# Seven half products in place of eight in the first MLP product of the last three blocks

## The chip, the cores and the metric

The kernel runs on 1 core of one Trainium2 chip. The metric is the device time of one execution in microseconds (us): 1153.07 us is the median of 3 runs of the kernel before, 1152.66 the lowest and 1155.45 the highest. The profile shows one further execution, taken by the hardware profiler.

The engines are named as the profile names them: PE is TensorE (matmuls), DVE is VectorE, ACT is ScalarE, POOL is GpSimd, SP is SyncE, which issues nearly all transfers (DMA). PSUM is the memory that PE writes to, in eight banks of 128 x 512 fp32.

## The reference, cut to what matters

Two layers, each an attention over 8 neighbours at distances 0, 2, ..., 14, and a mixer with an MLP, on x of 2048 rows and 512 columns:

```python
def A(x):                       # attention, 32 heads of 16
    q, k, v = split(x @ wqkv)
    logits = einsum(q, k[pos - 2 * w]) * 16 ** -0.5     # w = 0..7
    return einsum(softmax(logits), v[pos - 2 * w]) @ wo

def B(x):
    h = gelu(layernorm(x) @ w1)
    x1 = x + shift_quarters(h) @ w2
    return x1 + gelu(layernorm(x1) @ w3) @ w4           # w3 512 x 1792

x = x + A(layernorm(x));  x = x + B(layernorm(x))       # twice
```

The product with w3 is the one that the change computes in another way.

## The kernel before, in words

**Tiles and steps.** Each layer is done in 4 blocks of 512 rows, so there are eight steps n = 0..7, called blocks here; 4 to 7 are the second layer. A block goes through `p1_stream` (layer norm, product with wqkv, result to DRAM), `p2` (attention on DVE, four units of 8 heads, each a multiplication, a reduction, a softmax, a second multiplication and a tree of additions over 128 x 4096 elements), `p3` (product with wo, norm, product with w1, gelu), `p4` (product with w2, norm, result turned into the tile nT) and `p5` (the MLP). The work of up to three blocks is interleaved: `p5` of block n runs beside `p2` of block n+1 or n+2.

**Precision.** Every fp32 operand is split into an f16 high and an f16 low half, and a product is the sum of three f16 matmuls (`HLS`, l.40). So 128 columns of w3 times 512 rows, over 4 parts of the contraction, are 12 matmuls 128x512.

**The MLP, `p5` (l.1342).** A group of 3, 4 or 5 row tiles of 128 rows (5 in block 7; the fifth is done as a product 128 wide from a tile xt) passes 14 chunks of 128 columns of w3. Per chunk c: the first product (`up`, 12 matmuls into one of four PSUM banks "mm"); ACT's gelu in that bank and its copy as high half g; the low half by DVE, or by ACT and POOL; the second product (`down`, 3 matmuls for each row tile into four banks "acc"). w3 and w4 were split once by `big_pair` (l.932), stored to DRAM, and are loaded again for each block (`w<-w`) into 8 slots.

**Scales.** `p4` scales the normed rows to `SN` = 1024 before they become f16; each chunk of w3 has a scale of its own (`power_of`, l.503).

**What sets the order.** Every operation is recorded in a graph and then issued in one fixed list of numbers, `ORDER` (l.44): number // 4 is the operation, number % 4 the engine among its alternatives. `SLOTS` (l.220) gives each tile its place in memory. `plan` (l.311) replays the list, and `InOrder` (l.339) keeps each engine's instructions in exactly that order. No engine can pass over an instruction that waits. All instructions carry the line number of the one helper that issues them, l.348 before (l.372 after), so groups in the profile are told apart by tile names: `mm<-nT,w` is the first MLP product, `acc<-w,g` the second, `prod<-kv,q` attention, `mm<-wo_hl,oT` the product with wo.

The loop that sets the stages (l.1421 on) calls `p3`, `p4`, `p5` for n = 0..7 and, from n = 1 on, `p1_stream` and `p2` of n + 3 behind them; the list then moves the operations.

Of the kernel before, what the change touches and what calls it, by code (L numbers as in the profile page):

```python
# [1462 lines left out]
```

## Time and profile before

| | |
|---|---|
| median of 3 runs | 1153.07 us |
| the profiled execution's own time | 1153.17 us |
| its span | 1151.4 us |
| PE busy | 1138.7 us (99%) |
| DVE busy | 890.5 us (77%) |
| ACT busy | 600.7 us (52%) |
| POOL busy | 389.2 us (34%) |
| first MLP product `mm<-nT,w`, 128x512 | 1176 matmuls, 266.1 us |
| second MLP product `acc<-w,g`, 128x512 | 1302 matmuls, 298.1 us |

The profiled execution's own time is 1.8 us longer than its span, and both differ from the median by less than the runs do from each other. In the timeline a row is a run of like instructions: start, busy time, engine, operation, out<-in, shape, count; the brackets give idle time ahead of it and what ended that. In a list of groups the columns are: count | busy time in us, mean ns of one | idle time before them and its releasers. In the table of windows each engine has its busy time in a stretch, with the number of its instructions.

### The profile page before, as it was taken

The numbers are of one execution on the slowest core, as the hardware profiler recorded it, in microseconds if no ns is written. First come the engines' busy times: TensorE is split into PE (matmuls) and PEld (weight loads), VectorE is DVE, ScalarE is ACT, GpSimd is POOL, SyncE is SP. The second block draws the span as 40 slices with busy tenths as digits, with TensorE's granted clock in tenths as the row PEclk, the third lists the DMA queues.
The fourth block names the chain that finished last, engine by engine and source line by source line (L and its number), as shares of the span: only waits on it lengthen the run. The fifth ranks groups of instructions, "written<-read, shape, count | busy, mean of one in ns | idle before, by whom it ended". The sixth has DMA issues, their size and how long they took to land.

```text
span 1151.4 us, 15775 instructions
## 1 busy us (share of the span) xinstructions
PE 1138.7 (99%) x5661; PEld 558.4 (49%) x5661; DVE 890.5 (77%) x1077; ACT 600.7 (52%) x1156; POOL 389.2 (34%) x474
## 2 busy tenths in 40 slices
PE   8999999999999999999999999999999999999998
PEld 7555555555444444444444444444444444444554
DVE  6889989999998994699948998899835999324112
ACT  6776677556645555264644554635444544344232
POOL 4464354224325235402323563431512242323000
PEclk9999999999999999999999999999999999999999
DMA  7789987753875645862677679764457646533232
GB/s 247 235 251 286 276 260 242 247 206 101 247 201 148 209 102 146 241 201 73 187 186 252 187 194 227 180 169 133 116 163 200 221 108 197 124 83 101 74 110 73
DMA packets 237270, 207.35 MB, mean 180 GB/s; under 512 B 109388, under 2 KB 162884, under 8 KB 237192
## 3 DMA queue, kind: packets, MB, share of 16 engines
q1 hardware_dynamic: 236096, 205.51, 62.3%
q8 instruction: 44, 0.72, 0.2%
q10 hardware_dynamic: 1096, 0.85, 0.2%
q14 instruction: 34, 0.28, 0.1%
HBM read 141.03 MB, written 39.47 MB: 157 GB/s over the span
## 4 chain that ended last, share of the span: by engine, by line
PE 79%; DVE 10%; DMA 4%; issue 3%; POOL 2%; ACT 2%; SPq 0%; DVEq 0%; POOLq 0%; ACTq 0%
PE mm L348 55%; PE acc L348 25%; DVE prod L348 4%; DVE L L348 2%; DMA kvq_d<-ev 1%; POOL g L348 1%; DMA w<-in_A_x_dram 1%; DVE g L348 1%; DMA kv<-kvq_d 1%; DVE mx L348 1%; DMA w<-w 1%; DVE wq_hl L348 0%; DVE x L348 0%; SPq L348 0%; DVE f L348 0%
## 5 line engine op out<-in xcount | busy, mean ns | idle before, releaser
L348 PE MATMUL acc<-w,g 128*128 128x512 f16 x1302 | 298.1, 379 | 0.0
L348 PE MATMUL mm<-nT,w 128*128 128x512 f16 (+1 forms) x1344 | 294.8, 372 | 1.8 <-ACT ev L348 0.8
L348 POOL TENSOR_TENSOR g<-f,g 128x512 f16<-128x512 f32 (+1 forms) x123 | 173.0, 1412 | 330.8 <-ACT g L348 156.9
L348 ACT ACTIVATE mm<-mm,s_w 128x512 f32<-128x512 f32 (+2 forms) x158 | 98.2, 622 | 253.8 <-PE mm L348 253.3
L348 PEld LDWEIGHTS <-w 128*128 128x128 f16 x1512 | 140.9, 98 | 154.2 <-issue 3.3
L348 PEld LDWEIGHTS <-g 128*128 128x128 f16 x1398 | 136.7, 98 | 157.0 <-POOL g L348 0.2
L348 PE MATMUL mm<-wq_hl,xt 128*128 128x512 f16 x744 | 166.3, 379 | 0.6 <-DMA xt<-g 0.4
L348 PEld LDWEIGHTS <-xt 128*128 128x128 f16 x1008 | 98.6, 98 | 117.3 <-issue 1.4
L348 DVE TENSOR_REDUCE L<-prod 128x128 f32<-128x2048 f32 (+1 forms) x44 | 142.8, 3248 | 0.4
L348 DVE TENSOR_TENSOR prod<-kv,q 128x4096 f32<-128x4096 f32 (+1 forms) x27 | 100.8, 3736 | 10.5 <-DMA q<-kvq_d 5.9
L348 DVE TENSOR_TENSOR prod<-prod 128x1024 f32<-128x1024 f32 (+2 forms) x56 | 91.0, 1626 | 0.9
L348 PE MATMUL mm<-nT,w_hl 128*128 128x512 f16 x384 | 86.0, 379 | 0.5 <-DVE g L348 0.5
L348 PE MATMUL mm<-wo_hl,oT 128*128 128x512 f16 x384 | 86.0, 379 | 0.0
L348 PE MATMUL mm<-w_hl,h 128*128 128x512 f16 x384 | 85.5, 379 | 0.0
L348 DVE SCALAR_TENSOR_TENSOR g<-mm,c_g,g 128x512 f16<-128x512 f32 (+1 forms) x53 | 39.1, 742 | 56.5 <-ACT g L348 56.4
L348 DVE TENSOR_TENSOR prod<-kv,L 128x4096 f32<-128x4096 f32 (+1 forms) x21 | 77.5, 3690 | 0.4
L348 ACT ACTIVATE g<-mm,c_g 128x512 f16<-128x512 f32 (+1 forms) x112 | 74.5, 671 | 2.1
L348 PEld LDWEIGHTS <-oT 128*128 128x128 f16 x426 | 41.6, 98 | 49.6
L348 PE MATMUL acc<-wq_hl,xt 128*128 128x512 f16 x264 | 59.7, 379 | 0.0
L348 PEld LDWEIGHTS <-w_hl 128*128 128x128 f16 x384 | 37.5, 98 | 45.8 <-issue 0.8
L348 PEld LDWEIGHTS <-h 128*128 128x128 f16 x384 | 37.5, 98 | 45.2 <-DVE h L348 0.4
L348 DVE SCALAR_TENSOR_TENSOR x<-mm,s_wo,x 128x512 f32<-128x512 f32 x32 | 23.8, 747 | 41.2 <-PE mm L348 37.7
(245 smaller groups left out, 1364.1 us busy)
## 6 DMA issues: line engine op xcount, KB each, us to landing
w<-w SPq DMA_DIRECT2D x224, 256.0 KB, 3.9
kv<-kvq_d SPq DMA_DIRECT2D x62, 768.0 KB, 4.9
kvq_d<-ev SPq DMA_DIRECT2D x84, 256.0 KB, 4.0
w<-in_B_w_dram SPq DMA_DIRECT2D x28, 256.0 KB, 4.6
w<-g SPq DMA_DIRECT2D x28, 256.0 KB, 5.8
q<-kvq_d SPq DMA_DIRECT2D x28, 256.0 KB, 3.1
w<-in_A_x_dram SPq DMA_DIRECT2D x16, 256.0 KB, 5.1
x<-in_A_x_dram SPq DMA_DIRECT2D x16, 256.0 KB, 4.8
```

The costliest lines, as they stand in the source:

```text
L348: i = f(*a, **k).ins
```

## The change

For blocks 5, 6 and 7 (`FEW`) the first MLP product takes two chunks of w3 at once, a matrix of 256 columns by 512 parts of the contraction, halved in both directions, against rows halved in both directions. It is done in the form of Strassen and Winograd: seven products of halves in place of eight. Each product is 6 matmuls 128x256. The parts are:

- `lower_rows` and `turn_half`, in `p4`: four half-width subtractions of normed row tiles for each of two pairs of tiles, on DVE or POOL, their split into f16 halves, and their transposing DMAs into a tile S/U.
- `weight_sums`, behind block 3's MLP: w3 is read again, each pair of chunks gives two sums and differences of halves, these are split and stored in DRAM (`w34s`).
- `pair_up`, in `p5`: loads the two sums of a pair, and makes the seven products in two "mm" banks X and Y. ACT copies X out as s and, after an addition, half of Y as u; DVE does three additions 128x256 in PSUM (`Y += s`, `X += u`, `Y += s`), between which PE goes on writing to the same banks.
- The tiles S/U of block 5 lie in a "kv" slot and its weight sums in "w" slots; those of blocks 6 and 7 lie in the space of wq_hl, which is free after block 7's product with wqkv (`ends=wq_users` makes the DMAs that fill it wait for that).
- Scales: 512 in place of 1024 for the rows, and one scale for both chunks of w3 in a pair.
- `ORDER`, `SLOTS` and the place of 26 fill matmuls at the start (`KEEP`) are new throughout.

PE's instructions by kind: `mm<-nT,w` 128x512 from 1176 to 672; 882 matmuls 128x256 new (`nT,w` 336, `wq_hl` 168, `nT,wq_hl` 168, `kv,w` 126, `wq_hl,w` 84); fp32 turns `mm<-ident,f` from 100 to 120; `nT,minus_id` from 3 to 4. DMAs: 14 reads of w3, 14 writes and 42 loads of weights come, 12 transposes for S/U; five row tiles fewer are turned by DMA.

```diff
+    FEW = (5, 6, 7)
+    HOME = {5: ("kv", "f32", "f32", "f32", "f32", "w"), 6: ("nS", "ev", "xt", "ev", "xt", "ws"), 7: ("nS", "q", "o", "ev", "xt", "ws")}
...
-24 16 404 408 40 32 48 45 29 60 36 20 56 52 688 684 400 64 1788 69 72 1772 196 76 208 202 108 114 204 116 214 120 2316
+16 40 24 404 408 45 32 29 48 60 36 20 56 52 692 684 400 64 1772 69 77 196 72 202 108 114 121 204 116 80 210 214 86 126
...
-KEEP = {33: 26}
+KEEP = {22: 26}
...
+    def lower_rows(n, k, key, nr):
+        if k < 2 or k >= NT:
+            firsts[n][k] = nr
+            return
+        up, j, Q = firsts[n][k - 2], k - 2, D // 2
+        e, u = [Buf(b) for b in HOME[n][1:3]]
+        ev, uv = lambda: f32s(e), lambda: f32s(u)[:, :Q]
+        either(key, lambda E: E.tensor_sub(ev()[:, :Q], nr.t[:, :Q], up.t[:, :Q]), [nr, up], [(e, 0)])
+        either(key, lambda E: E.tensor_sub(ev()[:, Q:], nr.t[:, Q:], ev()[:, :Q]), [nr, (e, 0)], [(e, 1)])
+        either(key, lambda E: E.tensor_sub(uv(), up.t[:, Q:], ev()[:, Q:]), [up, (e, 1)], [u])
+        either(key, lambda E: E.tensor_sub(nr.t[:, :Q], nr.t[:, Q:], nr.t[:, :Q]), [], [nr])
...
+    def weight_sums(c, key):
+        either(key, lambda E: E.tensor_add(e.t[:, :Q], v(cd)[:, :Q], v(cd)[:, Q:]), [cd], [(e, 0)])
+        either(key, lambda E: E.tensor_sub(e.t[:, Q:], e.t[:, :Q], v(ab)[:, :Q]), [(e, 0), ab], [(e, 1)])
+        either(key, lambda E: E.tensor_sub(v(cd)[:, :Q], v(ab)[:, :Q], v(cd)[:, :Q]), [ab], [cd])
+        either(key, lambda E: E.tensor_sub(v(cd)[:, Q:], v(ab)[:, Q:], e.t[:, Q:]), [ab, (e, 1)], [cd])
...
+    def pair_up(n, c, key, w3):
+        X, Y_, s, u = Buf("mm"), Buf("mm"), Buf(HOME[n][3]), Buf(HOME[n][4])
...
+        product(X, 0, w3[0], 0, up, 0, True, B(nT, 0), [(X, [0, 1])])
+        product(X, 1, ws[0], 0, sv, 0, False, B(S, "S"), [(X, 1)])
+        product(Y_, 0, ws[0], 2, sv, 2, True, B(S, "S"), [(Y_, [0, 1])])
+        act(key, lambda: A.activation(s32(), X.t, AF.Copy), [(X, [0, 1])], [s],
+            also=[(DVE, lambda: V.tensor_copy(s32(), X.t), None)])
+        dve(key, lambda: V.tensor_add(y(0), y(0), s32()[:, :Q]), [s], [(Y_, 0)])
+        act(key, lambda: A.activation(u32(), y(0), AF.Copy), [(Y_, 0)], [u],
+            also=[(DVE, lambda: V.tensor_copy(u32(), y(0)), None)])
+        product(X, 0, w3[0], 2, up, 2, False, B(nT, 0), [(X, 0)])
+        product(X, 1, ws[1], 2, low, 2, False, B(nT, 1), [(X, 1)])
+        dve(key, lambda: V.tensor_add(x(1), x(1), u32()), [u], [(X, 1)])
+        product(Y_, 0, ws[1], 0, low, 0, False, B(nT, 1), [(Y_, 0)])
+        dve(key, lambda: V.tensor_add(y(1), y(0), s32()[:, Q:]), [s, (Y_, 0)], [(Y_, 1)])
+        product(Y_, 0, w3[1], 2, uv, 0, False, B(S, "U"), [(Y_, 0)])
+        return X, Y_
...
-            power(key, ss, ve, r, k, C1 / SN ** 2, EPS / SN ** 2, sums, C0, nb)
+            power(key, ss, ve, r, k, C1 / SX ** 2, EPS / SX ** 2, sums, C0, nb)
...
-                ps = Buf("mm")
+                ps = banks.get(c) if k0 == 0 and n in FEW else Buf("mm")
...
+        if n == 3:
+            for c in range(NP):
+                weight_sums(c, 3.0 + 0.1 * c)
```

Two places show how the list moves the work. First DVE, at the two ends of the attention of block 7. In the kernel before, these are the last row ahead of it (a cast of block 6's rows in `p3`), its first two rows, and its last rows with the first row behind it (`x<-mm,s_wo` takes up block 7's product with wo):

```order
L348 CAST g_262<-f_257 128x512
L348 TENSOR_TENSOR prod<-kv_274,q_305 128x4096
L348 TENSOR_REDUCE L_299<-prod 128x32x8
...
L348 TENSOR_SCALAR g_295<-o_297,c_o 128x512
L348 SCALAR_TENSOR_TENSOR g_294<-mm_72,c_g,g_294 128x512
L348 SCALAR_TENSOR_TENSOR g_295<-o_297,c_o,g_295 128x512
L348 SCALAR_TENSOR_TENSOR x_285,b_0_160<-mm_66,s_wo,x_285 128x512
```

In the changed kernel the same ends read as follows; rows `mm<-mm,f` are `pair_up`'s additions for block 5, rows `mm<-mm,ev` and `mm<-mm,xt` those for block 6:

```order
L372 TENSOR_TENSOR mm_68<-mm_68,f_284 128x256
L372 TENSOR_TENSOR mm_70<-mm_70,f_276 128x256
L372 TENSOR_TENSOR prod<-kv_291,q_288 128x4096
L372 TENSOR_REDUCE L_312<-prod 128x32x8
...
L372 TENSOR_SCALAR g_311<-o_316,c_o 128x512
L372 SCALAR_TENSOR_TENSOR g_311<-o_316,c_o,g_311 128x512
L372 TENSOR_TENSOR mm_68<-mm_68,ev_319 128x256
L372 COPY xt_317<-mm_68 128x256
L372 TENSOR_TENSOR mm_70<-mm_70,xt_317 128x256
```

Attention's first row now stands behind an addition of block 5's MLP, and additions of block 6's MLP follow its last row. Between the two ends the changed kernel has 106 rows, where it had 88.

Second PE, in the last pair of chunks of block 7. Before, each chunk is one run of twelve matmuls from nT, one from xt for the fifth row tile, and the second product into acc:

```order
L348 MATMUL mm_70<-nT_288,w_250 128x512
...
L348 MATMUL mm_68<-xt_304,w_250 128x128
...
L348 MATMUL mm_66<-nT_288,w_251 128x512
...
L348 MATMUL acc_273<-w_252,g_269 128x512
...
L348 MATMUL mm_70<-xt_304,w_251 128x128
```

After, X is mm_68 and Y is mm_66; S, U and the weight sums lie in wq_hl, nT is the tile of rows. Each matmul row shown stands for six like it (twelve for xt, three for each acc bank):

```order
L372 MATMUL mm_68<-nT_305,w_267 128x256
...
L372 MATMUL mm_68<-wq_hl 128x256
...
L372 MATMUL mm_66<-wq_hl 128x256
...
L372 MATMUL mm_72<-xt_320,w_267 128x128
...
L372 MATMUL mm_68<-nT_305,wq_hl 128x256
...
L372 MATMUL mm_66<-nT_305,wq_hl 128x256
...
L372 MATMUL acc_290<-w_299,g_286 128x512
...
L372 MATMUL mm_66<-wq_hl,w_266 128x256
```

The seven halves go to X and Y in turn; the fifth tile's product stands ahead of the second use of X, and a second product (acc, twelve matmuls) ahead of the last half into Y.

More of the change, by code (lines that the diff above doesn't have):

```diff
@@ L273, in pick, with __call__ @@
         return self.picks[-1]
-    def __call__(self, key, alts, r=(), w=(), after=()):
+    def __call__(self, key, alts, r=(), w=(), after=(), ends=()):
         o = Op()
@@ L303, in __call__ @@
                         st[1].append(o)
+        before.update(ends)
         before.discard(o)
@@ L449, in pe, with dma, turnstile @@
         return op(key, [(PE, fn, None)], r, w, after)
-    def dma(key, out, in_, r, w, after=(), by_act=False):
+    def dma(key, out, in_, r, w, after=(), by_act=False, ends=()):
         both = [(ACT, lambda: A.dma_start(out(), in_()), None), (SP, lambda: Y.dma_start(out(), in_()), None)]
-        return op(key, both if by_act else both[1:], r, w, after)
+        return op(key, both if by_act else both[1:], r, w, after, ends)
     before = {}
-    def turnstile(line, *a):
-        before[line] = [dma(*a, after=before.get(line, ()))]
+    def turnstile(line, *a, **k):
+        before[line] = [dma(*a, after=before.get(line, ()), **k)]
     GELU, EXP = "gelu", "exp"
@@ L485, in tile_mixer @@
     wo, w1, w2 = [keep(f"{n}_hl", [P, 2 * NC * D], F16) for n in ("wo", "w1", "w2")]
+    slots["nS"] = [wq.t[:, 3072 * k:3072 * (k + 1)] for k in range(3)]
+    slots["ws"] = [wq.t[:, 1024 * (9 + k):1024 * (10 + k)] for k in range(3)]
+    w34s_d = [[dram.tile([P, 2, 512], F16, name=f"w34s_{c}_{m}") for m in range(2)] for c in range(NP)]
+    wq_users = []
     def rows(ap, b, i):
@@ L872, in p1_stream @@
                 ways = [(0,), (1,)][:len(banks)]
-                pk(op(key + 0.01 * j, [(PE, lambda ps=ps, fn=fn: fn(ps), None) for ps in banks],
-                      [(xt, both), (wq, wq_all)], banks), *ways)
+                mm_op = pk(op(key + 0.01 * j, [(PE, lambda ps=ps, fn=fn: fn(ps), None) for ps in banks],
+                              [(xt, both), (wq, wq_all)], banks), *ways)
+                if n >= NB:
+                    wq_users.append(mm_op)
                 alts = []
@@ L944, in big_pair @@
         iv4 = Buf(None, inv_p.t[:, 4 * c:4 * c + 4])
-        power_of(key, (ss_p[c], list(range(4))), ss_p[c].t, 4, iv4, total=False)
+        power_of(key, (ss_p[c], list(range(4))), ss_p[c].t, 4, iv4, total=False, pairs=True)
         for m, t in enumerate(st):
@@ L1273, in group, with half_sums, either @@
         return ts + ([(n, NT - 1)] if n == N - 1 else [])
-    x2T = {}
+    x2T, x2S, firsts = {}, {}, {}
+    SU = lambda b: b.t.bitcast(F16) if b.kind == "kv" else b.t
+    S_of = lambda b: SU(b)[:, :2048]
+    U_of = lambda b: SU(b)[:, 2048:3072]
+    f32s = lambda b: f32v(b.t, D) if b.kind in ("xt", "oT") else b.t
+    def half_sums(n):
+        x2S[n], firsts[n] = Buf(HOME[n][0]), {}
+    def either(key, fn, r, w, ends=()):
+        return op(key, [(DVE, lambda: fn(V), None), (POOL, lambda: fn(G), None)], r, w, (), ends)
@@ new lines, in turn_half @@
+    def turn_half(key, nv, dst, cell, out, wd, rd, n):
+        hl = Buf("g")
+        hv = lambda a: halves(hl.t, wd)[:, a]
+        act(key, lambda: A.activation(hv(0), nv(), AF.Copy), rd, [(hl, 0)],
+            also=[(DVE, lambda: V.tensor_copy(hv(0), nv()), None)])
+        op(key, [(DVE, lambda: V.tensor_sub(hv(1), nv(), hv(0)), None),
+                 (POOL, lambda: G.tensor_sub(hv(1), nv(), hv(0)), None)], [*rd, (hl, 0)], [(hl, 1)])
+        op(key, [(SP, lambda: Y.dma_start_transpose(out(), hl.t[:, :2 * wd]), None)], [(hl, [0, 1])],
+           [(dst, cell)], (), wq_users if HOME[n][0] == "nS" else ())
@@ new lines, in weight_sums @@
+    def weight_sums(c, key):
+        op.stage = ("weight_sums", c)
+        Q = D // 2
+        ab, cd, e = Buf("w"), Buf("w"), Buf("f32")
+        v = lambda t: f32v(t.t, D)
+        for t, i in ((ab, 2 * c), (cd, 2 * c + 1)):
+            turnstile("sums", key, lambda t=t: v(t).rearrange("p (k f) -> p k f", k=NC),
+                      lambda i=i: w3_d[:, P * i:P * (i + 1)].rearrange("(k p) f -> p k f", p=P), [], [t])
+        either(key, lambda E: E.tensor_add(e.t[:, :Q], v(cd)[:, :Q], v(cd)[:, Q:]), [cd], [(e, 0)])
+        either(key, lambda E: E.tensor_sub(e.t[:, Q:], e.t[:, :Q], v(ab)[:, :Q]), [(e, 0), ab], [(e, 1)])
+        either(key, lambda E: E.tensor_sub(v(cd)[:, :Q], v(ab)[:, :Q], v(cd)[:, :Q]), [ab], [cd])
+        either(key, lambda E: E.tensor_sub(v(cd)[:, Q:], v(ab)[:, Q:], e.t[:, Q:]), [ab, (e, 1)], [cd])
+        sc = inv_p.t[:, 4 * c:4 * c + 1]
+        for m, (src, rd) in enumerate(((lambda: e.t, (e, [0, 1])), (lambda: v(cd), cd))):
+            hl = Buf("g")
+            hi, lo = [lambda a=a, hl=hl: halves(hl.t)[:, a] for a in range(2)]
+            hi_of(key, hi, src, sc, [rd, iv[c]], [hl])
+            rest_any(key, lo, src, sc, hi, [rd, iv[c]], hl, [(hl, 1)])
+            dma(key, lambda m=m: w34s_d[c][m], lambda hl=hl: halves(hl.t), [(hl, [0, 1])], [(w34, ("s", c, m))])
@@ new lines, in pair_up, with product, fn @@
+    def pair_up(n, c, key, w3):
+        Q = D // 2
+        nT, S = x2T[n][0], x2S[n]
+        ws = [Buf(HOME[n][5]), Buf(HOME[n][5])]
+        for m in range(2):
+            turnstile("w", key, lambda m=m: ws[m].t, lambda m=m: w34s_d[c][m].rearrange("p a f -> p (a f)"),
+                      [(w34, ("s", c, m))], [ws[m]], ends=wq_users if HOME[n][5] == "ws" else ())
+        X, Y_, s, u = Buf("mm"), Buf("mm"), Buf(HOME[n][3]), Buf(HOME[n][4])
+        B = lambda t, h: [(t, [(2 * h + k, a) for k in range(2) for a in range(2)])] if t is nT else [
+            (t, [(h, k) for k in range(2)])]
+        def product(bank, z, wt, kw, xv, kx, start, r, w):
+            def fn():
+                m, wv = 0, wt.t.rearrange("p (a k f) -> p a k f", a=2, k=NC)
+                for k in range(2):
+                    for a, b in HLS:
+                        T.matmul(bank.t[:, Q * z:Q * (z + 1)], wv[:, b, kw + k], xv(a, kx + k),
+                                 start=start and m == 0, stop=m == 5, skip_group_check=True)
+                        m += 1
+            return pe(key, fn, [wt, *r], w)
+        up = lambda a, k: blocks(nT.t, D)[:, a, k, :Q]
+        low = lambda a, k: blocks(nT.t, D)[:, a, k, Q:]
+        sv = lambda a, k: blocks(S_of(S), Q)[:, a, k]
+        uv = lambda a, k: U_of(S).rearrange("p (a k f) -> p a k f", a=2, k=2)[:, a, k]
+        s32, u32 = lambda: f32s(s), lambda: f32s(u)[:, :Q]
+        x, y = [lambda z, b=b: b.t[:, Q * z:Q * (z + 1)] for b in (X, Y_)]
+        product(X, 0, w3[0], 0, up, 0, True, B(nT, 0), [(X, [0, 1])])
[13 more added lines that the diff above has]
+        return X, Y_
@@ L1350, in p5 @@
         parts = [(0, min(K, NT))] + ([(NT, K)] if K > NT else [])
+        banks, w3s = {}, {}
         for c in range(NF):
             key = base + 0.001 * c
-            w3, w4 = Buf("w"), Buf("w")
+            if n in FEW and c % 2 == 0:
+                for m in range(2):
+                    w3s[c + m] = Buf("w")
+                    turnstile("w", key - 0.003, lambda m=m, c=c: w3s[c + m].t,
+                              lambda c=c, m=m: w34_d[c + m][:, 0].rearrange("p a f -> p (a f)"), [(w34, (c + m, 0))], [w3s[c + m]])
+                banks[c], banks[c + 1] = pair_up(n, c // 2, key, (w3s[c], w3s[c + 1]))
+            w3, w4 = w3s.get(c) or Buf("w"), Buf("w")
             if n < PLAIN:
@@ L1378, in up @@
                             m += 1
-                ups = [pe(key, up, [w3, (nT, [(k, a) for k in range(k0, k1) for a in range(2)])], [ps, (g, "new")], ups)]
+                if not (n in FEW and k0 == 0):
+                    ups = [pe(key, up, [w3, (nT, [(k, a) for k in range(k0, k1) for a in range(2)])], [ps, (g, "new")], ups)]
+                whole_ps = [(ps, [0, 1])] if n in FEW and k0 == 0 else [ps]
                 gv = lambda a, g=g, wd=wd: halves(g.t, wd)[:, a]
@@ L1383, in p5 @@
                 act(key, lambda pv=pv, sw=sw: A.activation(
-                    pv(), pv(), AF.Gelu_apprx_tanh, scale=sw), [s_w3], [ps], cls=GELU)
+                    pv(), pv(), AF.Gelu_apprx_tanh, scale=sw), [s_w3], whole_ps, cls=GELU)
                 act(key, lambda pv=pv, gv=gv, cg=cg: A.activation(
-                    gv(0), pv(), AF.Copy, scale=cg), [ps, c_g], [(g, 0)])
+                    gv(0), pv(), AF.Copy, scale=cg), [*whole_ps, c_g], [(g, 0)])
                 if c % VEC_G[n] == 0 or k0:
@@ L1392, in p5 @@
                     act(key, lambda pv=pv, t=t, wd=wd, cg=cg: A.activation(
-                        t.t[:, :wd], pv(), AF.Copy, scale=cg), [ps, c_g], [t])
+                        t.t[:, :wd], pv(), AF.Copy, scale=cg), [*whole_ps, c_g], [t])
                     gp(key, lambda gv=gv, t=t, wd=wd: G.tensor_sub(gv(1), t.t[:, :wd], gv(0)),
```

64 lines of the change are left out of this document (40 added, 24 removed), and 367 rows, old and new, of the table ORDER.

## The prediction

> **What bounds the kernel now.** I read the page first: the span, the engines' shares, the slices and the chain that ended last.
>
> ```profile
> span 1151.4 us, 15775 instructions
> PE 1138.7 (99%) x5661; PEld 558.4 (49%) x5661; DVE 890.5 (77%) x1077; ACT 600.7 (52%) x1156; POOL 389.2 (34%) x474
> PE   8999999999999999999999999999999999999998
> DVE  6889989999998994699948998899835999324112
> PEclk9999999999999999999999999999999999999999
> PE 79%; DVE 10%; DMA 4%; issue 3%; POOL 2%; ACT 2%; SPq 0%; DVEq 0%; POOLq 0%; ACTq 0%
> ```
>
> TensorE (PE) works from end to end at full clock and carries 79% of the chain. VectorE (DVE) is the second engine, full in some slices and nearly idle in the last ones. The profiled execution took 1153.17 us, 0.1 above the median of 1153.07, so I sum against 1153.17. Next the windows: PE's idle time by stage.
>
> ```profile
> core 0: us, PE busy (x) PEld busy (x) DVE busy (x) ACT busy (x) POOL busy (x), PEclk, DMA share, GB/s
> 0.00:250.00 250.00, 243.41 (x1368) 145.46 (x1369) 224.27 (x300) 167.42 (x356) 108.42 (x147) 1.00 0.80 249
> 350.00:1050.00 700.00, 698.58 (x3241) 316.73 (x3239) 543.34 (x613) 347.66 (x632) 242.60 (x276) 1.00 0.61 166
> 877.00:984.00 107.00, 106.01 (x492) 47.80 (x490) 102.59 (x92) 49.04 (x82) 27.47 (x28) 1.00 0.60 182
> 1056.00:1146.00 90.00, 89.89 (x542) 45.92 (x543) 20.66 (x38) 27.18 (x56) 0.00 (x0) 1.00 0.27 89
> ```
>
> From 350 to 1050 us PE lacks 1.4 us of 700; ahead of 250 it lacks 6.6. So what is taken off PE after 350 us comes off the time, unless another engine then comes late. The fourth row names the candidate: in the attention of block 7 (877 to 984) DVE has 102.59 us of work in 107, while in the tail (1056 to 1146) it has 20.66 in 90.
>
> **The change, part by part: PE.** Prices come from PE's timeline: distance from one group's start to the next, divided by the group's count.
>
> ```profile
> 1056.11 2.75 PE L348 MATMUL mm<-nT,w 128*128 128x512 f16 x12
> 1058.70 0.83 PE L348 MATMUL mm<-xt,w 128*128 128x128 f16 x12
> 1059.37 2.75 PE L348 MATMUL mm<-nT,w 128*128 128x512 f16 x12
> ...
> 228.79 2.11 PE L348 MATMUL mm<-nT,w 128*128 128x384 f16 x12
> 230.74 1.92 PE L348 MATMUL mm<-ident,prod 128*128 128x128 f32 x16
> ...
> 12.53 1.53 PE L348 MATMUL mm<-ident,f 128*128 128x128 f32 x12 [1.83 <-DVE f L348]
> 13.90 0.46 PE L348 MATMUL acc<-nT,oT 128*128 128x256 f32 x1
> ```
>
> 512 columns: 2.59/12 = 215.8 ns. 128 columns, each with its own weight load: 0.67/12 = 55.8. 384 columns: 1.95/12 = 162.5, which is exactly the straight line between the other two. A product 256 wide is not in the trace; that line gives 55.8 + 160/3 = 109.1 ns. The fp32 turns cost 1.37/12 = 114 ns.
>
> The first product of a pair of chunks was 24 matmuls of 512 columns, and becomes 42 of 256. Over 3 blocks of 7 pairs: 504 x 0.2158 = 108.8 us go, 882 x 0.1091 = 96.2 come. Some turns move from DMA to PE: 20 more fp32 turns (2.3 us) and one more 512-wide product (0.2). PE's own sum: -108.8 + 96.2 + 2.5 = **-10.1 us**. The 126 narrow products of the fifth row tile stay.
>
> The Trainium skill ("TensorE: Matmul & The Clock Gate", section "Back-to-back issue gap") speaks against this change: in a real stream of weight loads and matmuls it has about 81 ns at 128 columns and 131 at 512, so a narrow product would be dear. By it 504 x 131 = 66 us would go and, with 98 ns at 256 columns, estimated on its line, 86 would come: 20 us slower. The rows above disagree with both figures (55.8 and 215.8 ns), so the sum goes by the rows.
>
> **The change: DVE in block 7's attention.** Each pair adds three half-width additions on DVE, 63 in all, and each block eight half-width subtractions shared with POOL. Most of these land where DVE has room, but blocks 5 and 6 run beside the attention of block 7.
>
> ```profile
> 865.86 0.08 DVE L348 DVE_READ_ACCUMULATOR x<-mm,s_wo,x 128x1 f32 x1
> 872.86 0.43 DVE L348 CAST g<-f 128x512 f16<-128x512 f32 x1 [6.91 <-POOL f L348]
> 876.99 4.42 DVE L348 TENSOR_TENSOR prod<-kv,q 128x4096 f32<-128x4096 f32 x1 [3.71 <-DMA kv<-kvq_d]
> 963.09 0.41 DVE L348 TENSOR_TENSOR L<-L,mx 128x256 f32<-128x256 f32 x1
> 963.42 0.74 DVE L348 SCALAR_TENSOR_TENSOR g<-mm,c_g,g 128x512 f16<-128x512 f32 x1
> 982.96 0.74 DVE L348 SCALAR_TENSOR_TENSOR g<-o,c_o,g 128x512 f16<-128x512 f32 x1
> 988.04 4.26 PE L348 MATMUL mm<-wo_hl,oT 128*128 128x512 f16 x19
> ```
>
> Before, DVE waited over 10 us just ahead of this stretch, started at 876.99 and ended at 983.70; PE's product with wo needs the last piece, and began at 988.04, 4.34 us later. In the changed order DVE has 106 rows in the stretch instead of 88: 21 additions in PSUM and 3 half-width subtractions come, 2 casts, 1 low half and 3 scalings go to other engines or places.
>
> ```profile
> L348 DVE TENSOR_TENSOR mm<-L,mx 128x256 f32<-128x256 f32 x7 | 4.0, 568 | 0.6 <-ACT g L348 0.5
> L348 DVE CAST g<-f 128x512 f16<-128x512 f32 x2 | 0.8, 419 | 0.0
> L348 DVE TENSOR_SCALAR g<-o,c_o 128x512 f16<-128x512 f32 x4 | 1.9, 484 | 0.2
> oT<-g SPq DMA_TRANSPOSE x24, 4.2
> xt<-g SPq DMA_TRANSPOSE x20, 3.1
> ```
>
> An addition 128x256 in PSUM isn't in the trace. Nearest is the 0.41 at 963.09, start to start 0.33 (the next begins at 963.42); the dear end is 0.57, from the row whose output lies in PSUM. With whole durations: 24 x 0.41 - (2 x 0.42 + 0.74 + 3 x 0.48) = +6.8; by start to start: 24 x 0.33 - (2 x 0.35 + 0.67 + 3 x 0.41) = +5.3. So DVE needs 107.9 to 109.4 us for the stretch.
>
> Both engines can be counted from one point: the last addition ahead of the stretch (block 5's MLP) needs a product of PE. From that product's end to the first product with wo, PE's new order has 326 products of 512 columns, 348 of 256 and 12 turns: 70.4 + 38.0 + 1.4 = 109.7 us. DVE needs from there one addition (0.33 to 0.41), the stretch (107.9 to 109.4) and the transposing DMA (4.2; at least 3.1): 111.3 to 114.0. With 4.2 PE comes to wait 2.7 to 4.3 us; I take **+3.5**. Before, PE came at 988.04, when the landing (983.70 + 4.2) was just there. More idle on DVE (it had 107 - 102.6 = 4.4) or 0.57 for each addition (24 x 0.16 = 3.8) adds to it; a landing after 3.1 takes 1.1 off; PE waiting elsewhere in the stretch takes off as much.
>
> **Other hand-offs.** Within a pair: ScalarE (ACT) copies the first bank, DVE adds, ACT copies a half, DVE adds twice more, and PE writes to those banks again only then.
>
> ```profile
> L348 ACT ACTIVATE f<-mm,c_g 128x512 f32<-128x512 f32 x47 | 32.1, 683 | 1.0 <-DVE g L348 0.2
> L348 ACT ACTIVATE L<-L 128x256 f32<-128x256 f32 x32 | 13.2, 415 | 24.4 <-DVE L L348 24.3
> L348 SPq DMA_TRANSPOSE oT<-g x24: 1231/1237/2614, 304.7 to 983.7; - x24
> w<-w SPq DMA_DIRECT2D x224, 256.0 KB, 3.9
> ```
>
> The chain is 0.68 + 0.41 + 0.42 + 0.41 = 1.9 us a pair, 40 us in 21 pairs if PE did nothing meanwhile. In the new order of the last pair the copy (0.68) has one half (6 x 0.109 = 0.65) and the fifth tile's product (0.67) as cover, the addition and the half's copy (0.83) that product and two halves (1.98), the last addition (0.41) twelve matmuls with w4 (2.59). So I cost it at nothing; without the cover it is 1.9 us a pair.
>
> The sums of the rows lengthen the way to the first product that uses them: three subtractions (1.2) and two transposing DMAs more on SyncE's (SP) queue (1.24 each), 3.7 us a block at most. Behind the last w2 product stand 14.5, 16.7 and 5.8 us of PE work in blocks 5, 6 and 7; I take **+0.5** for all three, between 0 and 11. The transposes of blocks 6 and 7 also wait on SP, with later weight loads queued behind them, for the last product with the qkv weights; that ended at about 870 us before, and the rows they need come after 913, so the wait is over.
>
> ```profile
> 867.58 2.75 PE L348 MATMUL mm<-wq_hl,xt 128*128 128x512 f16 x12
> ...
> 912.93 2.75 PE L348 MATMUL mm<-w_hl,h 128*128 128x512 f16 x12
> ```
>
> The 70 added or repeated transfers of weights and their sums (14 reads of w3, 14 writes, 42 loads) are 256 KB each at 3.9 us to landing, issued ahead, at a DMA share of 0.61: nothing. The weight sums run in the middle on DVE, ACT and POOL (52% and 34% busy): nothing on PE. The seven small reductions of the shared scale (a few numbers wide) lie ahead of 250 us among PE's and DVE's waits: nothing.
>
> **The sum.** 1153.17 - 10.1 + 3.5 + 0.5 = 1147.1 us. A measurement of this kernel can tell about 0.3% (3.5 us) from no change, so "faster" begins below 1149.6.
>
> **The rivals.**
> - **Full gain.** The transposes land after 3.1, DVE's adds overlap as at 963.09, PE's waits elsewhere in the stretch absorb the rest, or the new order saves a few us of the 6.6 that PE lacks ahead of 250: 1141.5 to 1144.5. Against it: every count above has DVE late by 1.6 at least.
> - **DVE becomes the bound of blocks 5 to 7.** With the old 4.4 us of idle and 0.57 an addition PE waits 4.3 + 4.4 + 3.8 = 12.5 at the product with wo: 1153.17 - 10.1 + 12.5 + 0.5 = 1156. For it: 102.59 of 107. Against it: the 4.4 were in part waits for the first DMA and for PE, which a busier DVE doesn't see. Half of it is 1150 to 1156.
> - **Slower: hand-offs in pairs uncovered.** Place: PSUM banks between the seven products. Price 1.9 us a pair; it decides from 13.6 us on, seven of the 21 pairs bare. Half bare: 20 us, 1167. Against it: in the tail DVE has 20.66 us of work in 90 and answers at once, and beside attention the adds stand between steps of 4.4 us, where only the order protects them.
> - **Slower: narrow products cost more than their columns.** If a weight load of 98 ns did not overlap, 882 x 0.098 = 86 us: 1233. Against it: 55.8 ns at 128 columns. The skill's figures, above, would give about 1173 here.
>
> **Chances.** Forecast (1144.5 to 1149.6) 0.47, full gain 0.26, DVE bound (1149.6 to 1156.5) 0.18, hand-offs 0.07, narrow products 0.02. Faster 0.47 + 0.26 = 0.73, same 0.18, slower 0.09. The range 1141.5 to 1154.5 leaves out the two slower cases (0.09), the end of the DVE case (about 0.05) and a little below.
>
> **What would show it.** Groups of 256-wide f16 products at 109 ns start to start; PE's own work 10 us less; before block 7's product with wo an idle time of 2 to 5 us released by the transposed oT, behind a DVE stretch of 107 to 110 us with almost no idle; no idle of PE over 0.5 us ahead of products in pairs. It is wrong if PE's new waits sum to over 8 us, if they lie in the pairs, or if 256 columns take over 115 ns.

## The result

| | us | runs |
|---|---|---|
| before | 1153.53 median (1152.66 to 1155.45) | 4 |
| after | 1160.95 median (1160.0 to 1161.2) | 4 |
| predicted | 1147.1 (1141.5 to 1154.5) | |

The ratio after to before is 1.0061 [1.0043, 1.0078]: slower by 7.4 us, and 13.9 us above the forecast. The profiled execution of after took 1160.81 us, its span was 1159.1.

The page of the changed kernel, as far as it answers to the lines shown of before:

```profile
span 1159.1 us, 17044 instructions
PE 1133.6 (98%) x6060; PEld 596.7 (51%) x6060; DVE 939.8 (81%) x1172; ACT 638.3 (55%) x1233; POOL 437.5 (38%) x525
PE 71%; DVE 9%; DMA 9%; POOL 4%; issue 3%; ACT 3%; SPq 1%; POOLq 0%; DVEq 0%; ACTq 0%
```

PE is busy 5 us less and the span is 8 us longer. In the chain that ended last, transfers went from 4% to 9% and POOL from 2% to 4%. The windows say where:

```profile
core 0: us, PE busy (x) PEld busy (x) DVE busy (x) ACT busy (x) POOL busy (x), PEclk, DMA share, GB/s
0.00:250.00 250.00, 239.21 (x1329) 141.46 (x1330) 223.47 (x303) 158.78 (x340) 103.83 (x147) 0.99 0.82 250
350.00:650.00 300.00, 296.54 (x1376) 134.19 (x1375) 243.70 (x273) 149.31 (x265) 126.12 (x132) 1.00 0.68 191
350.00:1050.00 700.00, 690.61 (x3491) 340.71 (x3490) 576.77 (x673) 380.22 (x701) 273.76 (x301) 1.00 0.69 189
1062.00:1150.00 88.00, 88.00 (x677) 59.04 (x675) 35.21 (x71) 30.47 (x63) 3.12 (x6) 1.00 0.44 131
```

Ahead of 250 us PE now lacks 10.8 us (6.6 before), from 350 to 1050 it lacks 9.4 (1.4 before). In block 7's tail, where most of that block's pairs run and DVE has 35.21 us of work in 88, it lacks nothing.

For the sum by stages I use one measure for all kernels: the distance from each matmul's start to the next one's, less the median distance of matmuls of its kind. What is left over is PE's loss, waits and slower matmuls together. (It is larger than the windows' idle time, and the fall of PE's own sum larger than that of its busy time, since each group that is followed by a wait counts as busy 0.17 us beyond the distance of starts: 0.82 - 0.65 in the rows below.) Sums of such differences in us, and the medians of the runs (before was run again beside each group of them, with medians from 1152.79 to 1153.53):

| kernel | PE's own sum | 0-250 | 250-350 | 350-650 | 650-850 | 850-1060 | 1060-end | loss | median |
|---|---|---|---|---|---|---|---|---|---|
| before | 1133.4 | 9.7 | 0.7 | -0.1 | 0.7 | 1.5 | -0.1 | 12.4 | 1153.53 |
| after | 1123.2 | 16.6 | 1.5 | 4.0 | -0.1 | 8.1 | 0.2 | 30.3 | 1160.95 |
| x2_new_early | 1132.9 | 17.6 | 1.4 | 1.6 | 2.5 | -0.2 | 0.0 | 22.9 | 1162.90 |
| x4_old_to_385 | 1124.1 | 10.2 | 1.4 | 2.7 | -0.1 | 5.8 | 0.2 | 20.1 | 1153.62 |
| x5_no_sums | 1123.2 | 15.9 | 2.5 | 1.8 | 0.1 | 6.6 | 0.5 | 27.3 | 1159.16 |
| x12_one_place_stores | 1123.1 | 12.0 | 3.1 | 3.2 | -0.1 | 8.1 | 0.2 | 26.4 | 1155.87 |

So PE's own sum fell by 10.2, as forecast, and its losses rose by 17.9: 7.7 ahead of 350 us, 4.1 from 350 to 650, 6.6 in blocks 5 to 7, -0.5 elsewhere. None of the seven products runs in the first two stretches. In the first nothing of the change is executed but the seven small reductions of the shared scale and the moved fill matmuls; in the second `weight_sums` runs, from about 410 us on.

### The profile page after: what moved, and what is told of

It reads as the page before. It is cut to its first block, busy times and chain, and to the rows that moved or that the text cites. A ratio compares the mean times of both kernels' runs of the same rounds, so it can differ in the third digit from the quotient of the medians.

```text
span 1159.1 us, 17044 instructions
## 1 busy us (share of the span) xinstructions
PE 1133.6 (98%) x6060; PEld 596.7 (51%) x6060; DVE 939.8 (81%) x1172; ACT 638.3 (55%) x1233; POOL 437.5 (38%) x525
## 4 chain that ended last, share of the span: by engine, by line
PE 71%; DVE 9%; DMA 9%; POOL 4%; issue 3%; ACT 3%; SPq 1%; POOLq 0%; DVEq 0%; ACTq 0%
PE mm L372 48%; PE acc L372 23%; DVE prod L372 4%; DMA kvq_d<-ev 2%; POOL g L372 2%; DVE L L372 2%; DMA nT<-g 2%; DMA kv<-kvq_d 2%; DVE g L372 1%; DMA xt<-g 1%; SPq L372 1%; DVE mx L372 1%; DMA w<-in_B_w_dram 1%; ACT f L372 1%; POOL a L372 1%
## 5 line engine op out<-in xcount | busy, mean ns | idle before, releaser
L372 POOL TENSOR_TENSOR g<-f,g 128x512 f16<-128x512 f32 (+1 forms) x124 | 168.6, 1366 | 277.1 <-ACT f L372 120.0
L372 PE MATMUL mm<-nT,w 128*128 128x512 f16 (+2 forms) x1176 | 226.3, 343 | 7.4 <-DMA nT<-g 4.3
L372 PEld LDWEIGHTS <-w 128*128 128x128 f16 x1554 | 145.9, 98 | 118.5 <-issue 12.7
L372 DVE TENSOR_TENSOR prod<-kv,L 128x4096 f32<-128x4096 f32 (+1 forms) x19 | 71.5, 3763 | 0.2
L372 DVE TENSOR_TENSOR prod<-kv,acc 128x2048 f32<-128x2048 f32 (+1 forms) x24 | 67.3, 2812 | 0.1
L372 PE MATMUL acc<-wq_hl,xt 128*128 128x512 f16 x276 | 62.9, 379 | 2.0 <-DMA xt<-g 2.0
```

Of the source, the lines that this page charges most:

```text
L372: i = f(*a, **k).ins
```

## The price of the narrow products

Rows of the timeline of after, PE in block 6's MLP; each of the first two rows is one product of six matmuls 256 wide:

```profile
975.50 0.82 PE L372 MATMUL mm<-nT,wq_hl 128*128 128x256 f16 x6
976.15 0.82 PE L372 MATMUL mm<-wq_hl 128*128 128x256 f16 x6
976.80 2.75 PE L372 MATMUL acc<-w,g 128*128 128x512 f16 x12
...
998.92 2.75 PE L372 MATMUL mm<-wo_hl,oT 128*128 128x512 f16 x12
```

Twelve of them take 1.30 us from start to start, 108 ns each; the median of all is 109. That is the straight line between 128 and 512 columns, worth 504 x 0.2158 - 882 x 0.1091 = 12.5 us. By the estimate in the prediction, from the Trainium skill's figures for a real stream ("TensorE: Matmul & The Clock Gate", section "Back-to-back issue gap"), the change would be 20 us dearer on PE; the runs do not bear it out, with 108 ns at 256 columns, where 98 was estimated, and 215.8 at 512. The last row is the product with wo before which I expected PE to wait 3.5 us: it has no idle time ahead of it.

## Where PE waits now

PE's waits in after between 860 and 1010 us: engine, waited for, us in total, times, longest:

```profile
PE mm L372 <- DMA w<-w34s: 1.8, 2, 0.9
PE mm L372 <- DMA nT<-g: 1.6, 1, 1.6
PE mm L372 <- DMA wq_hl<-w34s: 0.7, 2, 0.4
PE mm L372 <- ACT ev L372: 0.7, 1, 0.7
PE mm L372 <- DVE mm L372: 0.7, 2, 0.4
```

There are eight waits and none is long: loads of weight sums, the last transpose of block 6's rows, ACT's copies, DVE's additions.

They decide who comes late at the product with wo. The window around the attention of block 7 in after:

```profile
883.00:996.00 113.00, 107.53 (x659) 63.97 (x657) 105.44 (x111) 65.97 (x114) 36.68 (x31) 1.00 0.75 215
```

From about 881.8, the end of the product that both engines were counted from, to the product with wo at 998.92 PE took 117 us: 109.8 of its own by the medians, as counted, and 7.4 lost on the way. DVE's stretch lasted 112.4 (883.25 to 995.63) with 105.1 of work, where 107.9 to 109.4 and almost no idle time were expected; its longest waits there were for PE (2.4 us in all) and for ACT (3.1). So the two engines held each other up in small steps, and PE came too late to wait for the transposed tile.

The largest single wait of the kernel is far from there, at block 0's hand-off to its MLP, which the change does not touch but whose steps stand in another order. In the kernel after:

```profile
198.23 2.75 PE L372 MATMUL mm<-w_hl,h 128*128 128x512 f16 x12
...
201.16 0.74 DVE L372 SCALAR_TENSOR_TENSOR f<-mm,s_w,f 128x512 f32<-128x512 f32 x1
...
205.65 1.16 POOL L372 TENSOR_TENSOR g<-f,g 128x512 f16<-128x512 f32 x1 [0.75 <-ACT g L372]
...
206.71 1.00 SPq L372 DMA_DIRECT2D w<-g  x2
207.82 1.95 SPq L372 DMA_TRANSPOSE nT<-g  x1
...
212.82 7.69 PE L372 MATMUL mm<-nT,w 128*128 128x384 f16 x36 [3.26 <-DMA nT<-g]
```

And the same chain in before:

```profile
190.61 7.93 PE L348 MATMUL mm<-w_hl,h 128*128 128x512 f16 x36
...
199.04 0.73 DVE L348 SCALAR_TENSOR_TENSOR f<-mm,s_w,f 128x512 f32<-128x512 f32 x1
...
203.58 1.16 POOL L348 TENSOR_TENSOR g<-f,g 128x512 f16<-128x512 f32 x1 [0.74 <-ACT g L348]
...
204.77 1.27 SPq L348 DMA_TRANSPOSE nT<-g  x1
```

Before, the three groups of products with w2 stand in one run of 36, and the transposing DMA goes out the moment POOL's half is ready (203.58 + 1.16 = 204.74). In the kernel after, the third group ends about 2 us later, since turns of attention stand between the groups, and the DMA stands behind two stores of weights: it goes out 3.05 us later. PE waits 3.26.

The wait costs more than its own length. By the trace's clock record the clock granted to PE is half for 3.41 us from 212.95 on, so the window behind the wait has a mean of 0.66:

```profile
213.00:218.00 5.00, 5.00 (x22) 2.62 (x21) 3.12 (x4) 1.72 (x3) 0.00 (x0) 0.66 0.97 330
```

The 36 products that follow take 7.69 us, where x12 below, which has no such wait, takes 6.01: 1.7 us more, and 4.9 with the wait. The traces of x2 (a wait of 3.28) and x11 (3.12) show the same 3.41 us at half clock behind it; that of x9 shows none behind its wait of 2.29.

## The experiments

My main theory after the result: the list is the cost. The new list hands work over later at several places ahead of 850 us, and would do so with eight products as well. Rivals are three: the new work itself (`weight_sums`, the pairs) makes PE wait; or the places in memory of the weight sums do; or the gain is there in block 7 alone and lost in blocks 5 and 6 beside attention. Each expectation says in its own words what each of them gives.

### x2_new_early: the new list, eight products

```diff
 before.py
-ORDER, SLOTS: before's throughout
+ORDER, SLOTS: the changed kernel's ahead of about 805 us, before's behind
```

> The kernel before (eight products in all blocks, no weight_sums), but everything issued ahead of about 805 us stands in the changed kernel's order and places; the rest is the order of before. Theory 1: the loss comes with the order, 1153.5 + 11 = 1164.5, between 1161 and 1166, with 3 us or more of PE idle between 300 and 600. Rival A (weight_sums makes the loss between 300 and 600): only the 7 us ahead of 250 come, 1159 to 1161, and idle of PE between 300 and 600 is under 1. Rival B: 1153 to 1155.

Measured: 1162.9, ratio 1.0079 [1.0063, 1.0095]. The computation is before's and yet the kernel is about 9 us slower (0.0079 of 1153). PE's waits between 175 and 260 us contain the one shown above:

```profile
PE mm L340 <- DMA nT<-g: 3.3, 1, 3.3
PE mm L340 <- POOL f L340: 1.4, 1, 1.4
```

So the list costs time by itself. Its loss ahead of 350 us (19.0) is about that of after (18.1). From 350 to 650 it loses 1.6, where after loses 4.0 and before nothing: there the list makes a part of the loss, and `weight_sums`, which this kernel lacks, may make the rest (see x5). What is exchanged here and in x4 is the order together with the places in memory and the place of the fill matmuls; only x12 below moves rows alone.

### x4_old_to_385: the old list ahead of block 2's MLP

```diff
 after.py
-ORDER, SLOTS: the changed kernel's throughout
+ORDER, SLOTS: before's first 1600 numbers (to about 385 us), the changed kernel's behind
```

> The changed kernel, but all that is issued ahead of about 385 us (before the first step of weight_sums) stands in the order and the places of the kernel before; nothing is put in between. Theory 1 (the new list loses 7 us by itself ahead of 350, where no step of the change stands yet): PE's idle time ahead of 350 falls from 18.1 to about 11, and the time to 1161 - 7 = 1154, between 1152.5 and 1156. Rival (that idle time only moves: PE is held by later work in any case): 1159 to 1161.

Measured: 1153.62 (12 runs), ratio 1.0008 [0.9998, 1.0019]. The same exchange from the other side takes 7.3 us off by the medians, 6.1 by the two ratios (2.4 either way), and the kernel with seven products is as fast as before. In the table its loss ahead of 350 us is 11.6, that of before 10.4. The main theory holds for this part. What still parts its profiled execution (1151.92 us) from the forecast of 1147.1 is mainly 2.8 us of loss from 350 to 650, 1.2 ahead of 350 and 0.8 in PE's own sum.

### x1_old_early and x10_old_to_185: other cuts

```diff
 after.py
-ORDER, SLOTS: the changed kernel's throughout
+x1: before's to about 770 us, with weight_sums's steps put between its rows
+x10: before's to about 185 us, the changed kernel's behind
```

> The changed kernel, but everything that is issued ahead of about 770 us stands in the order and the places of the kernel before; only the steps of weight_sums are put in between, behind the rows that they follow in the changed order. Blocks 5 to 7 are the changed kernel's. Theory 1 (the new list of order loses PE time ahead of 850 us by itself: 22.2 us of PE idle there against 11.1 before, and the seven products lose another 7.7 behind it): 1161 - 11 = 1150, between 1148 and 1153, with PE's idle time ahead of 850 back at 11 to 12. Rival A (the preparation, weight_sums with its loads on DVE, POOL and SP between 410 and 780, makes PE late in blocks 1 to 4): about 4 us of idle stay between 300 and 600, 1154 to 1156. Rival B (the loss is in the seven products): 1159 to 1161.

> The changed kernel with the order of before up to about 185 us only. Theory 1 in its strict form (each stretch of the new list loses by its own rows): PE's idle time ahead of 175 falls from 8.8 to about 7, that of 175 to 250 stays at 7 to 8, so 1159 to 1160. Rival (what is lost ahead of 185 delays block 0's second norm behind it): idle at 175 to 250 falls to 3 to 4, 1154 to 1156.

Measured: 1218.27, ratio 1.0565 [1.0547, 1.0583], and 1176.52, ratio 1.0208 [1.0187, 1.0230]. Both missed. PE's largest wait in the first, over the whole span:

```profile
PE mm L365 <- DMA w<-w: 30.0, 5, 19.1
```

and in the second, between 175 and 250 us:

```profile
PE mm L365 <- DVE mx L365: 5.8, 1, 5.8
PE acc L365 <- DVE prod L365: 3.7, 1, 3.7
```

In x1, with new steps between the rows of a finished list, loads of weights came up to 19.1 us late (the steps need w slots too, which is argued and not shown). In x10 PE waits for rows of attention on DVE; that the two lists had these rows at different points where they were joined is argued too. Neither tells the theories apart; they show how dear rows out of place are: 65 us and 23 more than x4_old_to_385.

### f7_block7_only and x8_block7_only: seven products in block 7 alone

```diff
-    FEW = (5, 6, 7)
+    FEW = (7,)
```

with before's list for blocks 0 to 6 and `weight_sums` put into it (in the second on POOL, where w slots were free, and with the changed kernel's order behind 1010 us).

> Seven products in block 7 alone, in the order of the kernel before, into which weight_sums and block 7's new steps are put at the places that they have in the changed kernel. Theory 1: PE's own sum falls by 168 x 0.2158 - 294 x 0.1091 = 4.2, less up to 1 for turns; block 7 lost 0.1 us in the changed kernel; 1153.5 - 3.5 = 1150, between 1149 and 1152. Rival A (weight_sums costs about 4 us in blocks 1 to 4): 1153 to 1155.

> Seven products in block 7 alone. All else stands in the order of the kernel before up to about 1010 us; the seven weight_sums are put, with their additions on POOL, where w slots are free (618 to 840 and 964 us); behind 1010 block 7's steps follow the changed kernel's order. Theory 3 (the products pay where DVE is idle and the order is kept): PE's sum falls by 168 x 0.2158 - 294 x 0.1091 = 4.2 less 0.5 for turns, block 7 lost 0.1 us in the changed kernel, so 1153.2 - 3.7 + 0.5 = 1150, between 1149 and 1151.5, faster than both kernels. Rival A (weight_sums costs 2 to 3 us wherever it stands): 1152 to 1153.5.

Measured: 1221.14, ratio 1.0575 [1.0553, 1.0598], and 1204.41, ratio 1.0452 [1.0438, 1.0467]. Both missed. PE's largest sum of waits is again for loads of w, 18.0 us in the first and 13.4 in the second. SyncE's queue in the first, from 1063 us on:

```profile
1063.55 2.61 SPq L354 DMA_TRANSPOSE nT<-g  x2
1066.42 34.47 SPq L354 DMA_DIRECT2D w<-w  x7
1100.94 0.90 SPq L354 DMA_DIRECT2D wq_hl<-w34s  x2
```

Seven loads held the queue 34 us, with the loads of the sums behind them. That is a part of the loss; the rest was not traced. What block 7 gains alone is open; in after its tail loses nothing (88.00 of 88), which speaks for it, but no run shows it.

### x3_own_slots and x3b_own_slots: the places of block 5's weight sums

```diff
-        ws = [Buf(HOME[n][5]), Buf(HOME[n][5])]
+        kind = "ws" if n == 5 and c >= 3 else HOME[n][5]
+        ws = [Buf(kind), Buf(kind)]
```

> The changed kernel with one edit: the weight sums of block 5's pairs 3 to 6 are loaded into the space of wq_hl, as those of blocks 6 and 7 are, instead of into the eight w slots. Theory 2 (the products of block 5 wait for their sums because SP's queue stands for 8 us at loads that wait for a w slot): the 2.5 us of PE idle at 882, 903 and 937 go, 1158.5. Rival C (the loads are late by their place in SP's fixed order, not for lack of a slot): 1160.5 to 1161, the waits stay.

> As the run with space of its own for block 5's weight sums, pairs 3 to 6, but every other tile keeps the place that it has in the changed kernel. Theory 2 (block 5's products wait for sums because their loads stand on SP's queue behind loads that wait for w slots): 2 to 2.5 us of PE idle between 880 and 940 go, and nothing comes behind 1000, so 1158.5; then the 10.8 us that the earlier run lost behind 1000 came from moving the other tiles. Rival: the loss behind 1000 stays, 1166 to 1170.

Measured: 1169.03, ratio 1.0131 [1.0110, 1.0153], and 1161.89, ratio 1.0076 [1.0063, 1.0089]. In the first, other tiles of w moved as well, and PE lost 7.7 us behind 1060, where after loses 0.2; waits between 1040 and 1167 us:

```profile
PE mm L365 <- DMA w<-w: 3.2, 1, 3.2
PE mm L365 <- DMA nT<-g: 2.9, 1, 2.9
```

In the second all others kept their places, and PE's waits from 860 to 1010 only changed their names:

```profile
PE mm L365 <- DMA wq_hl<-w34s: 2.5, 3, 1.3
PE mm L365 <- DMA nT<-g: 1.0, 1, 1.0
```

The waits for loads of sums are 2.5 us in all, as in after (1.8 and 0.7), though the sums of block 5's pairs 3 to 6 had space of their own: they are not late for want of a slot, and that rival falls. What is left is their place in SyncE's queue, which no run moved.

### x5_no_sums, x6_old_no_sums, x7_both: the weight sums

```diff
-            for c in range(NP):
-                weight_sums(c, 3.0 + 0.1 * c)
+            pass
```

x5 is after with this edit; `pair_up` then loads the split weights where it loaded their sums, so the sums of the weights are left out of the computation. x6 is x4 with this edit and x3b's, x7 is x4 with x3b's.

> The changed kernel in its own order without weight_sums; where their results are loaded, the split weights themselves are loaded, so the sums of the weights are left out of the computation, and all transfers and products behind them stay. Rival A in part (weight_sums costs 3 us between 400 and 650, as the order-only run had 0.5 us of idle at 450 to 650 and the changed kernel 3.7): 1157.5, between 1156.5 and 1158.5. Theory 1 alone (all idle ahead of 850 is the order's): 1160.5 to 1161.

> Old order to 385 us, space of its own for block 5's weight sums of pairs 3 to 6, and no weight_sums: the split weights are loaded in their place, so the sums of the weights are left out of the computation. If the parts add up: 1153.6 - 1.8 = 1151.8, between 1150.5 and 1152.5, with 2 us less idle between 385 and 650. What then still stands between this and 1153.2 - 10.2 = 1143 is idle time in blocks 5 and 6: 5 to 6 us between 850 and 1010, and 2 to 3 elsewhere.

> Two edits together: the old order to about 385 us, and block 5's weight sums of pairs 3 to 6 in their own space. If both theories hold and the parts add up: 1161 - 7 - 2.5 = 1151.5, between 1150 and 1153.5, a little ahead of the kernel before (1153.4). If the parts hide each other: 1154 to 1156.

Measured: 1159.16, ratio 1.0052 [1.0039, 1.0065]; 1154.86, ratio 1.0020 [1.0007, 1.0033]; 1154.13, ratio 1.0009 [0.9995, 1.0022]. x5's window from 350 to 650 us:

```profile
350.00:650.00 300.00, 298.65 (x1387) 135.30 (x1385) 239.42 (x265) 145.21 (x260) 99.42 (x111) 1.00 0.61 175
```

Without the sums PE lacks 1.35 us there instead of 3.46, POOL has 27 us less to do: what I costed at "nothing on PE" is 2.1 us, transfers of the sums included. The time, 1159.16, lies between what the two theories gave, so the list and the sums each hold a part of this stretch. x7 is as fast as x4: space of their own for the sums gains nothing with the old list either. x6 differs from x7 by the sums alone. By the measure of the table its loss from 350 to 650 is 1.0, where x7 has 4.1, yet it is not faster: 650 to 850 rises from 0.6 to 1.9 and 850 to 1060 from 6.0 to 8.6. What is saved early is lost again in blocks 5 and 6.

### x9_lo_on_dve: one wait of block 6 taken away

In x4 PE waits 1.38 us for the last transpose of block 6's rows. Rows of PE, DVE, POOL and SP there:

```profile
946.73 4.41 DVE L365 TENSOR_TENSOR prod<-kv,q 128x4096 f32<-128x4096 f32 x1
...
947.11 6.17 POOL L365 TENSOR_TENSOR g<-f,g 128x512 f16<-128x512 f32 x2 [0.63 <-ACT g L365]
...
952.19 1.24 SPq L365 DMA_TRANSPOSE nT<-g  x1
...
957.65 0.81 PE L365 MATMUL mm<-nT,wq_hl 128*128 128x256 f16 x6 [1.38 <-DMA nT<-g]
```

Two low halves on POOL take 6.17 us. So I moved the first of them to DVE, ahead of attention's product (a number of the list is operation times 4 plus the engine's place among its alternatives):

```diff
-14171   (its fourth alternative, POOL)
+14170   (its third, DVE, put ahead of prod<-kv,q)
```

> As the run in the old order to 385 us, with one operation moved: the low half of a row tile of block 6 (512 wide), which took POOL 5 us beside DVE's attention, is done by DVE ahead of the next attention row. Theory 4 (block 6's first products wait because POOL is slow beside DVE, which delays the last transpose of nT): the 1.4 us of PE idle ahead of mm<-nT,wq_hl at 957 go, 1152.2. Rival (the transposes for S and U on SP's queue are what is late): the idle time stays at 1 us or more, 1153.5.

Measured: 1154.41, ratio 1.0011 [1.0001, 1.0021]; not faster. Rows of the same place:

```profile
953.27 4.42 DVE L365 TENSOR_REDUCE L<-prod 128x256 f32<-128x4096 f32 x1
957.61 0.42 DVE L365 TENSOR_TENSOR mm<-mm,ev 128x256 f32<-128x256 f32 x1
...
958.12 0.38 ACT L365 ACTIVATE xt<-mm 128x256 f32<-128x256 f32 x1 [2.67 <-DVE mm L365]
...
959.70 0.82 PE L365 MATMUL mm<-nT,wq_hl 128*128 128x256 f16 x6 [2.29 <-ACT xt L365]
```

The transpose is no longer waited for. But DVE, with one row more ahead of attention, comes later to the pair's addition, which stands behind a reduction of 4.42 us; ACT waits 2.67 us for the addition and PE for ACT: 2.29 us in place of 1.38.

### x11_one_place and x12_one_place_stores: the hand-off of block 0

The three groups of products with w2 on PE, the step that takes up the third on DVE, and SP's queue:

```diff
 PE  mm_66<-w_hl,h x12
-PE  mm_70<-ident,prod x16
 PE  mm_68<-w_hl,h x12
-PE  mm_70<-oT,minus_id
 PE  mm_72<-w_hl,h x12
+PE  mm_70<-ident,prod x16
+PE  mm_70<-oT,minus_id
-DVE L_312<-prod (reduction)
 DVE f_276<-mm_72,s_w,f_276
+DVE L_312<-prod (reduction)
 x11, SP: w<-g, w<-w, kvq_d<-ev, w<-g, w<-g go behind nT<-g
 x12, SP: w<-g, w<-w, w<-g, w<-g go behind nT<-g; two kvq_d<-ev go ahead of it
```

Everything else is as in after.

> The changed kernel with its own list, except at one place, the hand-off from block 0's mixer to its MLP (190 to 213 us). There the changed list puts sixteen turns (1.75 us of PE) and one matmul between the three groups of block 0's products with w2, one reduction of attention (2.2 us of DVE) ahead of the step that takes up the third group, and three stores and loads (2.5 us of SP) ahead of the last transposing DMA; in this run the turns, the reduction and the five transfers around them stand behind those steps, as the list of before has it. Nothing is left out. Theory 'the new list costs time by itself, because hand-offs that were just in time now come late': the third product ends 2.0 us earlier, the last transpose is issued 2 to 3 us earlier, PE's wait of 3.26 us ahead of the first product with w3 falls to 0.5 to 1.5, and the time falls by 1.5 to 2.5 us, to 1158.5 to 1159.5. Rival 'what is saved there is given back, because attention on DVE sets the pace of the stretch': the wait falls as well, but the moved turns and the moved reduction make attention late, PE's waits between 215 and 350 rise by as much, and the time stays within 0.7 us of 1161. If the wait itself does not fall, the row argument on that place is wrong.

> As the run before it (one place, 190 to 213 us: the turns and the reduction behind the steps of block 0's mixer), but the two stores of attention's keys and queries, which that run pushed back behind the transposing DMA and which ScalarE then waited for (2.49 us at 219.49), are issued ahead of it, when their rows are ready; only stores and loads of weights stand behind it. Nothing is left out. Theory 'in-order queues: the wait was handed from one row to the next by my own move': PE's wait of 3.1 us at 220 goes as well, PE's idle time from 175 to 250 us falls from 7.8 to about 4.5, and the time from 1161 to about 1158. Rival 'attention sets the pace': the two waits go, and waits of the same sum (about 3 us) come up on PE behind VectorE's rows or at the next hand-off (330 to 340 us), and the time stays within 1 us of 1160.

Measured: 1159.54, ratio 1.0058 [1.0044, 1.0072], and 1155.87 (11 runs), ratio 1.0024 [1.0014, 1.0034]. In x11 the wait went, and another of the same size came at 220.23:

```profile
208.59 5.69 PE L365 MATMUL mm<-nT,w 128*128 128x384 f16 x34
...
211.75 0.53 SPq L365 DMA_DIRECT2D kvq_d<-ev  x1
...
219.49 0.69 ACT L365 ACTIVATE ev<-acc,s_kv 128x512 f32<-128x512 f32 x1 [2.49 <-DMA kvq_d<-ev]
...
220.23 3.35 PE L365 MATMUL acc<-w,g 128*128 128x512 f16 x9 [3.12 <-ACT ev L365]
```

ACT's copy needs the buffer `ev`, and the store that frees it still goes out at 211.75 (212.33 in after), behind what the move had left ahead of it, while PE came 4.2 us earlier. In x12, where the stores go out from 199.73 on, PE starts at 208.50 and goes on:

```profile
199.73 2.36 SPq L365 DMA_DIRECT2D kvq_d<-ev  x2
...
208.50 6.01 PE L365 MATMUL mm<-nT,w 128*128 128x384 f16 x36
...
217.27 2.10 PE L365 MATMUL acc<-w,g 128*128 128x512 f16 x9 [0.22 <-ACT ev L365]
```

The difference between after's ratio, 1.0061, and this one, 1.0024, is 4.3 us (about 2 either way, by their intervals; the profiled spans differ by 4.0). That is the size of the wait and the half clock behind it, 4.9. So one place of the list makes about half or more of what the list costs ahead of 385 us: 4.3 of 6.1 by the ratios, 3.0 of 6.5 by the losses ahead of 350 in the table. That attention would have taken the gain in any case is refuted for this place; 1.6 us of it come back as loss from 250 to 350 (3.1 against 1.5).

## Why the prediction was wrong, step by step

The time lies 13.9 us above the forecast. By the table, 7.7 of that are lost ahead of 350 us and 4.1 from 350 to 650, both counted at nothing; 2.6 in blocks 5 to 7 beyond the 4.0 that were counted; -0.5 elsewhere. PE's new losses sum to 17.9 us, where the prediction called itself wrong from 8 on.

- **PE's own sum, -10.1.** Right: -10.2.
- **The order ahead of 850 us.** This is the step that failed most. I counted it at nothing, and named it only as a possible gain ("saves a few us of the 6.6"). It costs 6.1 to 7.3 us ahead of 385 by x4; x2 shows about 9 with eight products. At block 0's hand-off the old list had a step just in time (204.74 to 204.77 in the rows of before); the new list missed it, and PE's wait of 3.26 us brought 1.7 us at half clock with it. The rest of the early loss was not traced to rows. The order of both kernels showed this place: the turns between the groups and the stores ahead of the transpose stood there to be read.
- **`weight_sums`, nothing on PE.** Failed by 2.1 us from 350 to 650. Without `weight_sums` the time falls by 1.8 us by the medians of x5 and after and by 1.0 by the ratios; the intervals overlap, so the profile's windows carry this, with x2, which has no sums and loses 1.6 there. In x6 the time doesn't fall at all.
- **The 70 added transfers, nothing.** Failed by about 2.5 us: that much of PE's waits in blocks 5 and 6 ends with a load of weight sums.
- **The wait at the product with wo, +3.5, and the sums of the rows, +0.5.** The mechanism was wrong, and that the size is near is luck: in x4, where the early part is as before, blocks 5 to 7 lose 4.3 us more than before, in after 6.6. None of it lies at the product with wo. I had let both engines run through to one meeting point; PE's own 109.7 us were right, but it lost 7.4 in small waits on the way, which I had named only as what "takes off as much". DVE, too, was idle for 7 us of its 112.4.
- **Hand-offs in pairs, nothing.** Nearly right. PE's waits for DVE's additions and ACT's copies come to 1.4 us in the list above, of the 40 that bare pairs would cost, though one is 0.7 where the prediction allowed 0.5.
- **The rivals.** "Slower" was priced at narrow products and bare hand-offs, not at the list, and nothing in my range stood for it.

What stays open: where the list loses the rest of its time ahead of 350 us; what is gained in block 7 alone with a list made for it; and whether the waits of blocks 5 and 6 can be removed, since those that x3b and x9 went for came back under another name.
